# Two reorderings in a three-stage mixer kernel: operands 5 and 6 of a pair, and the vector work of the first MLP

## The chip, the core and the metric

The kernel runs on one core of a Trainium2 chip. The metric is the device time of one execution in microseconds (us). TensorE multiplies matrices into PSUM; VectorE (DVE), ScalarE (ACT) and GpSimd (POOL) do the elementwise work; SyncE (SP) issues the DMAs. Each engine takes its instructions strictly in the order in which the program lists them, so an instruction that waits holds up all that stand behind it on its engine.

## What is computed

```python
def _attn_ref(q, k, v):                    # 4 batches, 8 heads, 576 positions, 64 wide
    scores = q @ k.T / sqrt(64)            # kept where 0 <= i - j < 64, else -1e9
    attn = exp(scores - max) / (sum + 1e-9)
    return attn @ v

def _moe_ref(x, g_ln, w_ch1, w_ch2):       # first MLP: 512 -> 2048 -> 512
    xn = (x - mean) / sqrt(var + 1e-6) * g_ln
    return x + maximum(xn @ w_ch1, 0) @ w_ch2

def _moe2_ref(x, w_tok1, w_tok2, w_ch1, w_ch2):
    u = x + token_mix(x)                   # along the 576 positions, 256 hidden
    return u + maximum(u @ w_ch1, 0) @ w_ch2   # second MLP: 512 -> 1536 -> 512
```

The output of each stage is the input of the next. Everything is float32, and the weights arrive as 64-bit numbers.

## The kernel before, in words

**Precision.** Each large product is made as three TensorE passes of a rounded type (`PASSES`): a number is split into a high half, written by ScalarE, and a low half, the difference, written by DVE or POOL (`split`, L105; `relu_split`, L364). The passes are high x high, high x low and low x high. Where the text says high half and low half, these two instructions are meant.

**Tiles and blocks.** The 2304 rows are 18 tiles of 128; three tiles make a block (384 columns of a transposed operand), so there are six blocks (`NBLOCKS`).

**First MLP** (`mlp_block`, L392). For block i, TensorE runs 16 steps f. A step is one `mm1` (L378: 12 matmuls into a hidden tile, whose two halves ScalarE and DVE then make, L365 and L366) and one `mm2` (L389: 9 matmuls) for the hidden tile of two steps before (`LAG` = 2). Behind the `mm1` of step f come the hooks of that step: all that prepares the next block. Blocks 1 to 4 take the hooks from `STEPS` (L702), where S, V, T and X stand for the work on one tile of the next block and a digit for which tile (3 is the first of the block after next):

- S (`tile_S`, L246): TensorE scores (L192), DVE maxima (L205), ScalarE exponentials (L213), into `f`.
- T (`tile_T_part`, L254): 16 DVE transposes, L260, of `f` into `pts`; T0*4 is four of them.
- V (`tile_PV`, L268): TensorE multiplies `pts` by the values (L285), DVE scales the result (L291); then `ln_scalar` (L301) centres the tile into `xh` on ScalarE.
- X (`xh_part`, L355): 16 DVE transposes, L359, of `xh` into `xhT`.

At a block's end `after` (L776) scales the three `xhT` into the next block's operand `xnt`.

**Early pieces.** 13 further weight pieces are fetched, narrowed, split and written back to DRAM meanwhile, in rows of the big tile `xs` that are still free (slots 9, 12 and 15). `EARLY` (L682) gives each slot the global steps (16 a block, block 1 starts at 0) at which a piece begins, and `PHASES` how many steps later each phase runs: load (SP), shrink (ScalarE), narrow (two DVE instructions), split (ScalarE and POOL), keep (SP).

**Token mixing** is a list written out by hand, `MIXING` (L56): u is `tok_up`, d is `tok_down` (TensorE, then a DVE addition, L856), r is DVE transposes, x is `x_step` (L897).

**Second MLP.** Two blocks at a time make a pair, three pairs in all. A group (`quad`, L942; six groups q per pair) computes two times two output blocks with seven products instead of eight: product k takes operand `xm[k]` (0 to 6), a sum or difference of the four quarters of the pair's input. The seven operands are made by `x_steps` (L874): four DVE subtractions `subs` (L877, into `t1`, `t2`, a quarter, and `t1` again) and seven splits `puts` (L107 high, L108 low). `subs[3]` overwrites `t1` for operand 6; `puts[5]` and `puts[6]` make operands 5 and 6. The list `lo` says which engine makes each low half. Products alternate between two PSUM banks, `pa` (0, 2, 4, 6) and `pb_` (1, 3, 5). Product 2 goes on in `pa`, which the ScalarE copy `s1` (L930) must have read first; likewise `s5` for product 3, and so on. Behind the products come the down products of the group before (L925, 36 matmuls), with ScalarE's and DVE's halves of the hidden tiles (L936, L939) between them.

```python
            product(pa, 0, a11)
            copy(s1, pa)
            job(0)
            product(pb_, 1, m1)
            copy(s5, pb_)
            job(1)
            product(pa, 2, m2, False)
```

`jobs` (L1000) holds what else is done in a group, by its place: job(k) stands behind product k for k up to 5, job(6) to job(9) behind the four pairs of hidden halves. Before the change the operands of the first pair are all made in the mixing list (x0 to x6), and those of the second and third pair in places 0 to 7 of the last group of the pair before (L1048 to L1056).

Of the kernel before, what the change touches and what calls it, by code (L numbers as in the profile page):

```python
# [12 lines left out]
U32 = mybir.dt.uint32  # L13
# [4 lines left out]
P = 128  # L18
B, H, S, D = 4, 8, 576, 64
DM = 512  # L20
# [4 lines left out]
T1 = 256  # L25
# [28 lines left out]


MIXING = ("u0 u1 y0 u2 d0 d1 y1 u3 d2 d3 y4 k4 r2 d4 r2 y2 k5 d5 r2 d6 y3 r2 d7 r2 t0 d8 r2 u4 w0 r2 u5 n2 t1 r2 x0 u6 x1 "  # L56
          "d9 x2 d10 u7 w1 n3 x3 d11 x4 d12 x5 d13 x6")


LOADS = ("q1 v0 q2 v1 g0 v2 w6")  # L60
# [12 lines left out]
def mixer_kernel(ctx, tc, qT, kT, v, g, wa1, wa2, tok1, tok2, wb1, wb2, out):  # L73
# [26 lines left out]
    def wslot(k, shape, name, dtype=F32R):  # L100

        return wp.tile(shape, dtype, tag=f"w{k}", name=name)
# [7 lines left out]
    def shrink(raw):  # L110

        h_ = raw.rearrange("p (n two) -> p n two", two=2)[:, :, 1].bitcast(F32)
        nc.scalar.activation(out=h_, in_=h_, func=AF.Prelu, scale=2.0 ** -112, alpha=2.0 ** 32)

    def narrow(pairs, psum=True):

        for d, r in pairs:
            w = r.rearrange("p (n two) -> p n two", two=2)
            low = ps_l.tile([P, DM], U32, tag="l", name="low")[:, 0:d.shape[1]] if psum else d
            nc.vector.tensor_scalar(out=low, in0=w[:, :, 0], scalar1=29, scalar2=None, op0=ALU.logical_shift_right)
            nc.vector.scalar_tensor_tensor(out=d, in0=w[:, :, 1], scalar=3, in1=low,
                                           op0=ALU.logical_shift_left, op1=ALU.bitwise_or)
        return [d.bitcast(F32) for d, _ in pairs]
# [280 lines left out]
    with tc.manual_schedule():  # L408
# [270 lines left out]

        EARLY = {9: (-1, 10), 12: (0, 10, 15, 26), 15: (0, 11, 16, 27, 32, 37, 43)}  # L682
        PHASES = ((0, piece_load), (2, piece_shrink), (2, piece_narrow), (3, piece_split), (4, piece_keep))
        pieces = [t1_piece(0), t1_piece(1), t2_piece(0), t2_piece(1), rest_piece()]
        pieces += [w2_piece(q, k) for q in range(HALF - 2) for k in range(2)]
        starts = sorted((g_, x) for x, gs in EARLY.items() for g_ in gs)
        at = collections.defaultdict(list)
        for (g_, x), piece in zip(starts, pieces):
            for d, fn in PHASES:
                at[g_ + d].append((d, fn, x, piece))  # L690

        def early_hooks(g_, hooks):
            for d, fn, x, piece in sorted(at[g_], key=lambda e: -e[0]):
# [4 lines left out]
                else:  # L698
                    hooks.append(call)


        STEPS = ("T0*4", "T0*4", "", "V0 S1", "X0*6 T1*2", "T1*8", "T1*6", "V1 S2 X0*5", "X0*5 T2*4", "T2*8", "T2*4 X1*4",  # L702
                 "V2 S3 X1*5", "X1*7", "X2*8", "X2*8 T3*8")
        done = collections.Counter()


# [190 lines left out]
        def x_step(k):  # L897
            {1: subs0[0], 2: subs0[1]}.get(k, lambda: None)()
            puts0[k]()
            {3: subs0[2], 5: subs0[3]}.get(k, lambda: None)()  # L900

        for op in MIXING.split():
            k = int(op[1:])
# [92 lines left out]
        for p in range(PAIRS):  # L996
            old = acc
            for q in range(HALF):
                n = p * HALF + q
                jobs = collections.defaultdict(list)  # L1000
                if p == 0:
                    if q == 0:
                        for k, t in ((1, 14), (3, 15), (5, 16), (9, 17)):
                            jobs[k].append(lambda t=t: tok_down(t))
                        jobs[9] += [lambda: load_w2(2), lambda: load_w2(3)]
                        more = wslot(15, [P, 2, 2 * DM], "more", U32)
                        wide = {}

                    def w2_raw(q2):
                        for k in range(2):  # L1010
                            f = q2 + k * HALF
                            nc.sync.dma_start(out=more[:, k], in_=wb2[f * P:(f + 1) * P, :].bitcast(U32))

                    def w2_narrow(q2, k):
                        if k == 0:
                            wide[q2] = ap.tile([P, 2, DM], U32, tag="p", name=f"wide{q2}")
                        narrow([(wide[q2][:, k], more[:, k])], False)

                    def w2_split(q2):
                        w2[q2], t_ = wslot(W2_SLOT[q2], [P, 2, 2, DM], f"w2_{q2}"), wide.pop(q2).bitcast(F32)  # L1020
                        for k in range(2):
                            split(w2[q2][:, k, 0], w2[q2][:, k, 1], t_[:, k], nc.gpsimd)

                    for m in range(2):
                        q2 = HALF - 2 + m
                        if q == m:
                            jobs[9].append(lambda q2=q2: w2_raw(q2))
                        if q == m + 1:
                            for k in range(2):
                                jobs[6].append(lambda k=k: shrink(more[:, k]))  # L1030
                                jobs[7 + 2 * k].insert(0, lambda q2=q2, k=k: w2_narrow(q2, k))
                        if q == m + 2:
                            jobs[5].append(lambda q2=q2: w2_split(q2))
                if 2 <= n + 1 < PAIRS * HALF:
                    jobs[0].append(lambda n=n: load_w1(n + 1))
                if p < PAIRS - 1:
                    if q == 0:
                        ux = qkv.rearrange("p a b n -> p (a b n)").rearrange("p (i c n) -> p i c n", i=2, n=N)
                        per = (6, 7, 7, 6, 6, 0)
                        todo = [(i, k) for i in range(2) for k in range(16)]  # L1040

                    def turn(m, p=p, ux=ux):
                        for i, k in todo[:m]:
                            block_transpose(ux[:, i], 2 * (p + 1) + i, k)
                        del todo[:m]
                    for k in range(per[q]):
                        jobs[5 + k % 5].append(lambda: turn(1))
                    if q == HALF - 1:  # L1048
                        tx = wslot(15, [P, 2, 2, N], f"tx{p}", F32)
                        subs, puts = x_steps(*(ux[:, i, c:c + 2] for i in range(2) for c in (0, 2)), tx[:, 0], tx[:, 1],  # L1050
                                        [nc.gpsimd, nc.vector] * 4)
                        jobs[0] += subs[:2]
                        jobs[3].append(subs[2])
                        for k, m in ((4, 0), (4, 1), (5, 2), (5, 3), (5, 4), (6, 5), (7, 6)):
                            jobs[k].append(puts[m])
                        jobs[6].insert(0, subs[3])  # L1056
                if q == 1:
                    acc = []
                    jobs[3].append(lambda p=p, acc=acc: acc.extend(new_acc(p)))
                for m, k, js in ((0, 8, (3, 4)), (0, 9, (5, 0)), (1, 0, (1, 2))):  # L1060
                    if q == m and p > 0:
                        jobs[k] += [lambda j=j, p=p, old=old: store(2 * TPB * (p - 1) + j, old[j]) for j in js]
                quad(n, old if q == 0 else acc, jobs)
# [54 lines left out]
```

## Time and profile before

| | us |
|---|---|
| median of 3 runs (lowest, highest) | 817.39 (815.83, 817.45) |
| the profiled execution | 816.4 |
| its span | 814.5 |
| TensorE busy | 798.4 |
| DVE, ScalarE, POOL busy | 535.5, 332.2, 174.7 |

The first MLP with the attention takes the time from the start to about 477 us, token mixing to about 518 us, and the second MLP the rest. TensorE's granted clock was 1.00 in every stretch of 20 us but the last (0.99). In a timeline, a row is a run of like instructions: start, time, engine, line, operation, output and inputs, and the count; in brackets, the idle time of the engine just before and what ended it. Ends of matmuls are modelled, so one run may end a little after the next has begun.

### The profile page before, as it was taken

What the parts mean: (1) busy time and instruction counts of PE and PEld (TensorE: products, weight loads), DVE (VectorE), ACT (ScalarE), POOL (GpSimd) and SP (SyncE); (2) the same over time, 40 slices, a digit from 0 to 9 for tenths busy, and PEclk for the clock granted to TensorE, in tenths of its full rate; (3) what the DMA queues carried; (4) which work ended last, traced back from release to release, by engine and by line L of the source; (5) the groups of instructions that cost most, each with busy time, mean ns of one, the idle gap of its engine ahead of it and who ended that gap; (6) DMA issues with size and microseconds to landing.
All of it is one profiled execution on the core that took longest, in us unless ns stands there. A gap on an engine that the chain in (4) does not pass through costs nothing.

```text
span 814.5 us, 13225 instructions
## 1 busy us (share of the span) xinstructions
PE 798.4 (98%) x4914; PEld 708.9 (87%) x4914; DVE 535.5 (66%) x1326; ACT 332.2 (41%) x852; POOL 174.7 (21%) x181
## 2 busy tenths in 40 slices
PE   8999999999999999999999999899999999999998
PEld 6788888889889888888999888789988998898997
DVE  5898697887889688777677337766465544732223
ACT  6887634444343344342254532333242222522221
POOL 4655401011001000000033933301231000400000
PEclk9999999999999999999999999999999999999999
DMA  9888324342322323121059516166240734235202
GB/s 339 271 293 273 101 93 135 111 168 85 110 78 78 111 85 110 35 81 56 1 135 354 201 40 245 52 245 232 93 176 4 257 117 156 91 112 218 109 1 78
DMA packets 35152, 112.67 MB, mean 138 GB/s; under 512 B 5008, under 2 KB 6544, under 8 KB 31632
## 3 DMA queue, kind: packets, MB, share of 16 engines
q1 hardware_dynamic: 34944, 111.56, 39.6%
q8 instruction: 39, 0.64, 0.3%
q10 hardware_dynamic: 144, 0.26, 0.1%
q14 instruction: 25, 0.20, 0.1%
HBM read 88.87 MB, written 22.41 MB: 137 GB/s over the span
## 4 chain that ended last, share of the span: by engine, by line
PE 76%; DVE 14%; ACT 5%; issue 2%; DMA 0%; POOL 0%; DVEq 0%; ACTq 0%
PE acca L389 18%; PE ha L378 17%; PE accb L925 15%; PE prod L916 15%; DVE pts L260 4%; PE th L839 3%; PE td L853 2%; PE o L285 2%; ACT f L213 2%; PE s L192 2%; DVE xhT L359 2%; DVE hTa L366 1%; PE accb L1074 1%; DVE xm L108 1%; PE pt L228 1%
## 5 line engine op out<-in xcount | busy, mean ns | idle before, releaser
L378 PE MATMUL ha<-xnt,wa 128*128 128x384 f32 x1152 | 216.9, 337 | 0.8 <-POOL wa L108 0.5
L389 PE MATMUL acca<-wa,hTa 128*128 128x512 f32 x864 | 215.8, 396 | 0.3 <-DVE hTa L366 0.3
L378 PEld LDWEIGHTS ha<-xnt,wa 128*128 128x128 f32 x1152 | 203.9, 188 | 9.5 <-DVE xnt L343 1.2
L389 PEld LDWEIGHTS acca<-wa,hTa 128*128 128x128 f32 x864 | 159.2, 188 | 33.3 <-issue 2.4
L925 PE MATMUL accb<-w,hx 128*128 128x512 f32 x612 | 142.2, 390 | 0.0
L925 PEld LDWEIGHTS accb<-w,hx 128*128 128x128 f32 x612 | 114.6, 188 | 23.2
L365 ACT ACTIVATE hTa<-ha 128x384 fp32r<-128x384 f32 x96 | 46.8, 488 | 186.7 <-PE ha L378 182.8
L366 DVE SCALAR_TENSOR_TENSOR hTa<-ha,hTa 128x384 fp32r<-128x384 f32 x96 | 53.2, 554 | 68.6 <-ACT hTa L365 67.8
L260 DVE STREAM_TRANSPOSE pts<-f 32x256 f32<-32x256 f32 x192 | 83.7, 436 | 3.1
L933 POOL TENSOR_TENSOR s<-s,s 128x384 f32<-128x384 f32 x18 | 18.2, 1014 | 228.3 <-ACT s L930 228.3
L916 PE MATMUL prod<-xm,w1b 128*128 128x384 f32 x324 | 59.9, 336 | 5.8 <-ACT s L930 5.8
L930 ACT ACTIVATE s<-prod 128x384 f32<-128x384 f32 x72 | 35.0, 492 | 68.1 <-PE prod L916 62.4
L916 PEld LDWEIGHTS prod<-xm,w1b 128*128 128x128 f32 x324 | 56.2, 188 | 7.4 <-ACT s L930 7.2
L939 DVE SCALAR_TENSOR_TENSOR hx<-s,hx 128x384 fp32r<-128x384 f32 x54 | 33.1, 616 | 44.8 <-ACT hx L936 44.7
L933 DVE TENSOR_TENSOR s<-prod,s 128x384 f32<-128x384 f32 x36 | 20.1, 557 | 63.4 <-PE prod L916 63.4
L359 DVE STREAM_TRANSPOSE xhT<-xh 32x128 f32<-32x128 f32 x192 | 57.8, 301 | 2.8
L936 ACT ACTIVATE hx<-s 128x384 fp32r<-128x384 f32 x54 | 27.9, 523 | 67.9 <-PE accb L925 66.7
L108 POOL TENSOR_TENSOR wa<-tmp,wa 128x512 fp32r<-128x512 f32 x32 | 41.5, 1312 | 34.0 <-ACT wa L107 32.3
L213 ACT ACTIVATE f<-f,mx 128x128 f32<-128x128 f32 x120 | 46.3, 387 | 1.2 <-DVE mx L205 1.2
L309 POOL TENSOR_SCALAR mv<-mv 128x1 f32<-128x1 f32 x13 | 2.6, 197 | 181.9 <-ACT xhT L308 181.8
L916 PE MATMUL prod<-xm,w1a 128*128 128x384 f32 x216 | 40.9, 336 | 0.0
L916 PEld LDWEIGHTS prod<-xm,w1a 128*128 128x128 f32 x216 | 38.0, 188 | 0.1
(150 smaller groups left out, 955.5 us busy)
## 6 DMA issues: line engine op xcount, KB each, us to landing
xs<-in_wa SPq DMA_DIRECT2D x32, 512.0 KB, 4.6
w1b<-kept SPq DMA_DIRECT2D x16, 1024.0 KB, 7.2
w1a<-kept SPq DMA_DIRECT2D x16, 768.0 KB, 4.8
qkv<-in_v SPq DMA_DIRECT2D x28, 256.0 KB, 3.1
qkv<-in_wb SPq DMA_DIRECT2D x12, 512.0 KB, 4.5
kept<-w1b SPq DMA_DIRECT2D x6, 1024.0 KB, 8.2
kept<-w1a SPq DMA_DIRECT2D x6, 768.0 KB, 6.2
xs<-in_wb SPq DMA_DIRECT2D x8, 512.0 KB, 4.7
```

The lines of the kernel that those rows point to most:

```text
L108: lo_engine.tensor_tensor(out=dst_lo, in0=src, in1=dst_hi.bitcast(F32), op=ALU.subtract)
L213: nc.scalar.activation(out=f_[:, h], in_=f_[:, h], func=AF.Exp, scale=-1.0, bias=mx[:, h], accum_out=sm[:, h])
L260: nc.vector.transpose(out=s_[32 * b:32 * b + 32, :, 32 * a:32 * a + 32], in_=f_[32 * a:32 * a + 32, :, 32 * b:32 * b + 32])
L359: nc.vector.transpose(out=uts[t][32 * b:32 * b + 32, :, 32 * a:32 * a + 32], in_=s_)
L365: nc.scalar.activation(out=dst_hi, in_=src, func=AF.Relu)
L366: nc.vector.scalar_tensor_tensor(out=dst_lo, in0=src, scalar=0.0, in1=dst_hi.bitcast(F32), op0=ALU.max, op1=ALU.subtract)
L378: nc.tensor.matmul(h_, lhsT=w[:, a, c * P:(c + 1) * P], rhs=src[c][:, b], start=n == 0, stop=n == 3 * KD - 1)
L389: nc.tensor.matmul(acc[j], lhsT=t_[:, a, j * P:(j + 1) * P], rhs=ws[f][:, 2 + b], start=f == first and n == 0, stop=f == last and n == 2)
L916: nc.tensor.matmul(dst, lhsT=w_[:, a, c * P:(c + 1) * P], rhs=xm[m][:, c, b], start=first and n == 0, stop=n == 5, skip_group_check=True)
L925: nc.tensor.matmul(acc[j], lhsT=hx[role][:, a, (j % TPB) * P:(j % TPB + 1) * P], rhs=w2[q][:, k, b], start=q == 0 and role in ("21", "12") ...
L930: nc.scalar.activation(out=dst, in_=src, func=AF.Copy)
L933: eng.tensor_tensor(out=dst, in0=x, in1=y, op=ALU.add)
```

## The change

The mixing list loses x5 and x6. For every pair, `subs[3]`, `puts[5]` and `puts[6]` are put at places 0, 1 and 3 of the first group that uses the operands, ahead of what stands there. For pairs two and three, operand 4 moves from place 5 to place 6 of the last group before, and the low halves of operands 5 and 6 change engines (5 from DVE to POOL, 6 from POOL to DVE). The buffer `more`, which takes the memory of `ut`, is taken when it is first loaded, since `ut` is now read in that group. In the first MLP the steps of S and V stay where they are, transposes move between steps, an early piece's numbers name the step of its shrink and narrow (loaded two steps before), and its split is done at least one step later and not before step 4 of a block.

```diff
@@ -54,7 +54,7 @@
 
 
 MIXING = ("u0 u1 y0 u2 d0 d1 y1 u3 d2 d3 y4 k4 r2 d4 r2 y2 k5 d5 r2 d6 y3 r2 d7 r2 t0 d8 r2 u4 w0 r2 u5 n2 t1 r2 x0 u6 x1 "
-          "d9 x2 d10 u7 w1 n3 x3 d11 x4 d12 x5 d13 x6")
+          "d9 x2 d10 u7 w1 n3 x3 d11 x4 d12 d13")
 
 
 LOADS = ("q1 v0 q2 v1 g0 v2 w6")
@@ -679,15 +679,16 @@
 
 
 
-        EARLY = {9: (-1, 10), 12: (0, 10, 15, 26), 15: (0, 11, 16, 27, 32, 37, 43)}
-        PHASES = ((0, piece_load), (2, piece_shrink), (2, piece_narrow), (3, piece_split), (4, piece_keep))
+        EARLY = {9: (1, 13), 12: (2, 12, 18, 28), 15: (2, 12, 18, 28, 34, 40, 45)}
         pieces = [t1_piece(0), t1_piece(1), t2_piece(0), t2_piece(1), rest_piece()]
         pieces += [w2_piece(q, k) for q in range(HALF - 2) for k in range(2)]
         starts = sorted((g_, x) for x, gs in EARLY.items() for g_ in gs)
         at = collections.defaultdict(list)
         for (g_, x), piece in zip(starts, pieces):
-            for d, fn in PHASES:
-                at[g_ + d].append((d, fn, x, piece))
+            late = max(4 - g_ % FA, 1)
+            for n, (d, fn) in enumerate(((-2, piece_load), (0, piece_shrink), (0, piece_narrow), (late, piece_split),
+                                         (late + 1, piece_keep))):
+                at[g_ + d].append((n, fn, x, piece))
 
         def early_hooks(g_, hooks):
             for d, fn, x, piece in sorted(at[g_], key=lambda e: -e[0]):
@@ -699,8 +700,8 @@
                     hooks.append(call)
 
 
-        STEPS = ("T0*4", "T0*4", "", "V0 S1", "X0*6 T1*2", "T1*8", "T1*6", "V1 S2 X0*5", "X0*5 T2*4", "T2*8", "T2*4 X1*4",
-                 "V2 S3 X1*5", "X1*7", "X2*8", "X2*8 T3*8")
+        STEPS = ("T0*4", "T0*4", "", "V0 S1 X0*6", "T1*6", "T1*8", "T1*2 X0*5", "V1 S2 X0*5", "T2*8", "T2*8", "X1*9",
+                 "V2 S3 X1*7", "X2*6", "X2*10", "T3*8")
         done = collections.Counter()
 
 
@@ -897,7 +898,7 @@
         def x_step(k):
             {1: subs0[0], 2: subs0[1]}.get(k, lambda: None)()
             puts0[k]()
-            {3: subs0[2], 5: subs0[3]}.get(k, lambda: None)()
+            {3: subs0[2]}.get(k, lambda: None)()
 
         for op in MIXING.split():
             k = int(op[1:])
@@ -1000,21 +1001,24 @@
                 jobs = collections.defaultdict(list)
                 if p == 0:
                     if q == 0:
+                        subs, puts = subs0, puts0
                         for k, t in ((1, 14), (3, 15), (5, 16), (9, 17)):
                             jobs[k].append(lambda t=t: tok_down(t))
                         jobs[9] += [lambda: load_w2(2), lambda: load_w2(3)]
-                        more = wslot(15, [P, 2, 2 * DM], "more", U32)
-                        wide = {}
+                        wide, more = {}, []
 
                     def w2_raw(q2):
+                        if not more:
+                            raw = wslot(15, [P, 2, 2 * DM], "more", U32)
+                            more.extend(raw[:, k] for k in range(2))
                         for k in range(2):
                             f = q2 + k * HALF
-                            nc.sync.dma_start(out=more[:, k], in_=wb2[f * P:(f + 1) * P, :].bitcast(U32))
+                            nc.sync.dma_start(out=more[k], in_=wb2[f * P:(f + 1) * P, :].bitcast(U32))
 
                     def w2_narrow(q2, k):
                         if k == 0:
                             wide[q2] = ap.tile([P, 2, DM], U32, tag="p", name=f"wide{q2}")
-                        narrow([(wide[q2][:, k], more[:, k])], False)
+                        narrow([(wide[q2][:, k], more[k])], False)
 
                     def w2_split(q2):
                         w2[q2], t_ = wslot(W2_SLOT[q2], [P, 2, 2, DM], f"w2_{q2}"), wide.pop(q2).bitcast(F32)
@@ -1027,12 +1031,15 @@
                             jobs[9].append(lambda q2=q2: w2_raw(q2))
                         if q == m + 1:
                             for k in range(2):
-                                jobs[6].append(lambda k=k: shrink(more[:, k]))
+                                jobs[6].append(lambda k=k: shrink(more[k]))
                                 jobs[7 + 2 * k].insert(0, lambda q2=q2, k=k: w2_narrow(q2, k))
                         if q == m + 2:
                             jobs[5].append(lambda q2=q2: w2_split(q2))
                 if 2 <= n + 1 < PAIRS * HALF:
                     jobs[0].append(lambda n=n: load_w1(n + 1))
+                if q == 0:
+                    for k, fn in ((0, subs[3]), (1, puts[5]), (3, puts[6])):
+                        jobs[k].insert(0, fn)
                 if p < PAIRS - 1:
                     if q == 0:
                         ux = qkv.rearrange("p a b n -> p (a b n)").rearrange("p (i c n) -> p i c n", i=2, n=N)
@@ -1048,12 +1055,11 @@
                     if q == HALF - 1:
                         tx = wslot(15, [P, 2, 2, N], f"tx{p}", F32)
                         subs, puts = x_steps(*(ux[:, i, c:c + 2] for i in range(2) for c in (0, 2)), tx[:, 0], tx[:, 1],
-                                        [nc.gpsimd, nc.vector] * 4)
+                                        [nc.gpsimd, nc.vector, nc.gpsimd, nc.vector, nc.gpsimd, nc.gpsimd, nc.vector])
                         jobs[0] += subs[:2]
                         jobs[3].append(subs[2])
-                        for k, m in ((4, 0), (4, 1), (5, 2), (5, 3), (5, 4), (6, 5), (7, 6)):
+                        for k, m in ((4, 0), (4, 1), (5, 2), (5, 3), (6, 4)):
                             jobs[k].append(puts[m])
-                        jobs[6].insert(0, subs[3])
                 if q == 1:
                     acc = []
                     jobs[3].append(lambda p=p, acc=acc: acc.extend(new_acc(p)))
```

## Rows read from the trace of the kernel before

**Rows 1.** The page, the span and its part 1: busy us, share of span, instructions.

```profile
span 814.5 us, 13225 instructions
...
PE 798.4 (98%) x4914; PEld 708.9 (87%) x4914; DVE 535.5 (66%) x1326; ACT 332.2 (41%) x852; POOL 174.7 (21%) x181
```

**Rows 2.** Busy time by stretch: blocks 1 to 4, length first, then engines' busy us, clock, DMA.

```profile
106.30:182.63 76.33, 74.43 (x530) 66.24 (x528) 63.60 (x194) 33.39 (x103) 9.63 (x12) 1.00 0.37 120
182.63:257.13 74.50, 74.09 (x529) 66.32 (x528) 62.41 (x195) 31.40 (x99) 7.38 (x10) 1.00 0.29 96
257.13:330.90 73.77, 73.77 (x529) 66.14 (x528) 60.91 (x193) 30.15 (x97) 6.10 (x9) 1.00 0.25 85
330.90:404.67 73.77, 73.77 (x503) 66.30 (x502) 55.35 (x167) 23.84 (x75) 2.23 (x6) 1.00 0.15 47
```

**Rows 3.** Timeline of TensorE, block 1.

```profile
137.81 1.15 PE L285 MATMUL o<-qkv,pts 128*64 128x64 f32 x30 [1.58 <-DVE pts L260]
...
180.89 1.90 PE L389 MATMUL acca<-wa,hTa 128*128 128x512 f32 x7 [0.32 <-DVE hTa L366]
```

**Rows 4.** Timeline of DVE, block 1, steps 4 to 7.

```profile
127.03 0.56 DVE L366 SCALAR_TENSOR_TENSOR hTa<-ha,hTa 128x384 fp32r<-128x384 f32 x1 [5.12 <-ACT hTa L365]
127.50 1.86 DVE L359 STREAM_TRANSPOSE xhT<-xh 32x128 f32<-32x128 f32 x6
...
135.07 2.69 DVE L260 STREAM_TRANSPOSE pts<-f 32x256 f32<-32x256 f32 x6
```

**Rows 5.** Timeline of ScalarE, block 1, end of step 3.

```profile
125.10 0.38 ACT L213 ACTIVATE f<-f,mx 128x128 f32<-128x128 f32 x1
...
125.49 1.14 ACT L107 ACTIVATE xs<-xs 128x512 fp32r<-128x512 f32 x2
```

**Rows 6.** Timeline of DVE, end of block 1.

```profile
174.11 2.52 DVE L359 STREAM_TRANSPOSE xhT<-xh 32x128 f32<-32x128 f32 x8
...
180.28 0.56 DVE L366 SCALAR_TENSOR_TENSOR hTa<-ha,hTa 128x384 fp32r<-128x384 f32 x1
```

**Rows 7.** Timeline of TensorE, second MLP.

```profile
523.60 2.37 PE L916 MATMUL prod<-xm,w1b 128*128 128x384 f32 x12 [2.29 <-ACT s L930]
...
597.48 1.23 PE L916 MATMUL prod<-xnt,w1a 128*128 128x384 f32 x6
...
604.79 8.36 PE L925 MATMUL accb<-w,hx 128*128 128x512 f32 x36
613.00 1.23 PE L916 MATMUL prod<-xnt,w1a 128*128 128x384 f32 x6
...
616.74 3.42 PE L916 MATMUL prod<-xm,w1b 128*128 128x384 f32 x18 [1.47 <-ACT s L930]
...
711.79 3.39 PE L916 MATMUL prod<-xm,w1b 128*128 128x384 f32 x18 [1.44 <-ACT s L930]
```

**Rows 8.** Timeline of ScalarE around the first groups of pairs one and two.

```profile
522.32 0.84 ACT L107 ACTIVATE xm<-t0x 128x768 fp32r<-128x768 f32 x1 [2.81 <-DVE t0x L877]
...
599.79 0.49 ACT L930 ACTIVATE s<-prod 128x384 f32<-128x384 f32 x1 [0.55 <-PE prod L916]
...
612.21 0.85 ACT L107 ACTIVATE xm<-tx 128x768 fp32r<-128x768 f32 x1 [2.79 <-DVE tx L877]
...
616.20 0.87 ACT L930 ACTIVATE s<-prod 128x384 f32<-128x384 f32 x2 [2.31 <-DVE hx L939]
```

**Rows 9.** Timeline of DVE around the start of pair two.

```profile
602.41 0.95 DVE L877 TENSOR_TENSOR qkv<-qkv 128x768 f32<-128x768 f32 x1
604.90 2.23 DVE L108 TENSOR_TENSOR xnt<-tx,xnt 128x768 fp32r<-128x768 f32 x1 [1.54 <-ACT xnt L107]
...
612.96 3.14 DVE L939 SCALAR_TENSOR_TENSOR hx<-s,hx 128x384 fp32r<-128x384 f32 x3
```

**Rows 10.** Timeline of POOL, last group of pair one.

```profile
604.46 1.86 POOL L108 TENSOR_TENSOR xnt<-qkv,xnt 128x768 fp32r<-128x768 f32 x1
606.28 2.56 POOL L108 TENSOR_TENSOR xm<-tx,xm 128x768 fp32r<-128x768 f32 x1
```

## What the change does to the time

> **What bounds the kernel now.** I read the busy shares first, then the stretches of the first MLP block by block, then TensorE's own timeline for the idle time in brackets, and only then, for each gap, the queues of the engines named in it. The busy shares [rows 1] say that TensorE works for 798.4 of 814.5 us: whatever the change does, it can only take from the remaining 16 us, and part of those are the start and the last stores, which it does not touch. A change of order pays only where TensorE waits.
>
> There are two places. In the first MLP the four blocks that also prepare the next block do the same TensorE work, but last 76.33, 74.50, 73.77 and 73.77 us [rows 2]. The last two have no idle TensorE time, so 73.77 is the price of the work, and the first two lose 2.56 and 0.73 us, 3.29 in sum. The timeline names the waits of the first: the probabilities-times-values products (L285) wait 1.58 us for the DVE transposes of their tile (L260), and the last second-layer products (L389) 0.32 us for a hidden tile [rows 3]. The bracketed idle time is a little less than the loss, since matmul ends are modelled and overlap the next start.
>
> The second place is the third product of the first group of each of the three pairs of the second MLP. It writes the bank that the copy s1 has to read first, and it waits 2.29, 1.47 and 1.44 us for that ScalarE copy [rows 7]. In a group without a wait the seven products take (604.79 - 597.48) / 7 = 1.044 us each. The second pair begins at 613.00, so its third product was due at 615.09 and started at 616.74: 1.65 us lost, 0.18 over the bracket. With the same 0.18 the three are 2.47, 1.65 and 1.62, together 5.74 us. Why the copy is late stands in two queues. For the first pair ScalarE stood 2.81 us waiting for a DVE subtraction into t0x, then made the high half of operand 6, and only then came to the copies. For the second it waited 2.79 us for the subtraction into tx, and then 2.31 us more for DVE's low halves [rows 8], three of which took 3.14 us and ended at 616.1 [rows 9]. So the work of operands 5 and 6, queued ahead of the group, delays a copy that needs neither.
>
> **The change, part by part.** *Operands 5 and 6.* The subtraction into t1, both halves of operand 5 and both of operand 6 leave the end of the pair before (for the first pair, the mixing list) and go behind products 0, 1 and 3 of the group that uses them; nothing is added. Ahead of the group, ScalarE loses two activations of 0.84 us [rows 8] and DVE a subtraction and a low half, 0.95 us each when alone and over 2 beside a POOL instruction [rows 9]. The copies then wait for TensorE only: 5.74 us come free.
>
> What takes their place is worked out for the second pair, with the group starting at 613.00. The subtraction follows DVE's last low half and runs beside products 1 and 2. The copy of product 1 started 2.31 us after the group's start in the undisturbed group (599.79 against 597.48) [rows 7, 8], so at 615.31; after it, 0.39 later since it is pipelined (0.87 for two against 0.49 for one), ScalarE makes high half 5 until 615.70 + 0.84 = 616.54. The copy s2 queued behind it is due at 616.35 and slips by 0.1; it ends at 616.95, and product 4, which overwrites that bank, comes at 617.18: hidden with 0.2 to spare. POOL's low half 5 takes 1.86 or 2.56 us [rows 10] and so ends at 618.5 or 619.1, and product 5 wants it at its second matmul, 613.00 + 5 x 1.044 + 0.17 = 618.4. The stall is 0.1 or 0.7 us. I take 0.1, because the 1.86 belongs to the half that started 0.44 us ahead of the DVE instruction beside it (which took 2.23 in place of 0.95), and the 2.56 to one that started while DVE held on [rows 9, 10]; here low half 5 starts first. Low half 6 on DVE follows the addition of product 3 and that POOL instruction: 618.5 + 0.95 = 619.4, when product 6 wants it at its second matmul (613.00 + 6 x 1.044 + 0.17 = 619.4): nothing, with 0.7 as the bound if low half 5 takes 2.56. The third pair is alike, so 0.2 us come back. Behind high half 6 on ScalarE stands the copy of product 4, and behind low half 6 on DVE the addition of product 5; both are due after 618.4 and wait for nothing but their product. In the first pair a token-mixing product (`tok_down`, six matmuls) stands behind each of products 1, 3 and 5, so product 5 comes later still by two of these: nothing comes back. The net of this part is 5.74 - 0.2 = 5.5 us.
>
> The Trainium skill's page "SBUF — State Buffer" (section "Who interferes with whom") says that GpSimd and a DVE instruction with two inputs in SBUF lock the port they share for a whole instruction, and that the one which started first is not slowed. The rows agree (1.86 beside 2.23); by that rule the stall at product 5 is the 0.1, by a sharing of the port it would be the 0.7, and the total 1.2 us more over two pairs.
>
> *Low halves change engine, operand 4 goes one step later.* Low half 5 goes to POOL and 6 to DVE. Operand 4 moves behind the first high half of the products; its POOL low half queued behind two others anyway (the second of them ran to 606.28 + 2.56 = 608.84 [rows 10]), and product 4 of the next group comes at 617.18. Nothing. *The buffer `more`* is taken later, with its loads, which stand at the same place of SP's queue: nothing.
>
> *Order of the first MLP's DVE work.* In step 3 DVE stood 5.12 us waiting for a ScalarE high half [rows 4], which was queued behind the exponentials and two early splits of 1.14 us [rows 5]. Then came 1.86 us of X0 transposes, and tile 1's 16 transposes ended at 137.76, after TensorE had arrived at 137.81 - 1.58 = 136.2. The change puts the six X0 transposes into that idle time, ahead of the wait, and moves the splits behind the high half. The low half then ends at about 127.59 - 1.14 = 126.5; 16 transposes at 2.69 / 6 = 0.45 us and two low halves of 0.57 between them give 126.5 + 7.2 + 1.1 = 134.8, or 1.4 us before TensorE comes. If the idle time did not cover X0, the 1.86 would come back and the stall would be 0.5. The 1.58 us of this wait go, and the 0.73 of the second block, which has the same steps and two pieces. At the block's end the late low half starts at 180.28, behind eight X2 and eight T3 transposes [rows 6]. Steps 11 to 14 now hold 23 X transposes in place of 28, so it comes 5 x 0.315 = 1.6 us sooner, against a loss of at most 2.56 - 1.58 = 0.98: gone, and the lower bound is that all of it stays. *Early pieces.* Their 13 loads, shrinks, narrows, splits and keeps are the same in number; narrows move by one step at most. Three splits now meet in step 4 of the first block, 3 x 0.57 = 1.7 us of ScalarE and their POOL halves, behind the high half that mattered and while DVE still transposes; the next high half slips, but its DVE partner is behind those transposes. The keeps, one or two steps later on SP, have the operand loads of step 7 behind them, three steps off. Nothing. This part is worth 3.3 us, at least 0 and at most 3.3.
>
> **The sum.** 5.5 + 3.3 = 8.8 us. The profiled execution took 816.4 (span 814.5), so it would take 807.6. It lies 1.0 below the median of the runs shown, 817.39; against that, 808.6.
>
> **Rivals.** *A, the low halves collide:* low half 5 takes 2.56, low half 6 follows it, and products 5 and 6 wait 0.7 us more in two pairs. The row of 2.56 speaks for it, the free POOL at that time against it. 810.0. *B, the first MLP's stall stays:* the transposes of tile 1 end as late as before because the exponentials, not X0, set them. The 1.4 us margin is against it. 808.6 + 3.3 = 811.9. *C, the change only moves the waits:* what product 2 gains comes back at product 5, because operand 5 is late there by as much (5.7 us), and transposes brought forward in one step are paid for in a later one (3.3 us): 817.4. For it speaks that no work is taken away, against it that DVE and ScalarE stood idle where the work now goes. *D, slower:* the chain of operands 5 and 6 does not run beside the products but in a line. Subtraction 2.2, high half 0.84, low half 2.56, and for operand 6 high 0.84 and low 2.2 follow one another, 8.6 us; only the 3.1 us of three products cover it. TensorE then stands 5.5 us in each pair, 16.5 in sum against the 0.2 forecast: 808.6 + 16.3 = 824.9. It is slower once the stall is over 0.1 + 8.8 / 3 = 3.0 us a pair. Against it: the steps are on three engines, and each finds its own free in the rows.
>
> **How the numbers follow.** Forecast 0.70 (808.6), A 0.10, B 0.09, C 0.05, D 0.06. A difference under 0.2%, 1.6 us, about the spread of the runs shown, can't be told from none. Faster: 0.70 + 0.10 + 0.09 = 0.89; same: C, 0.05; slower: D, 0.06. The range takes in the runs' spread below (808.6 - 1.8) and A and B above with a little spread: 806.8 to 812.2.
>
> **What would show it.** Right: the four blocks at 73.8 us each; no wait of L285 for L260 after the first block; the third product of each pair's first group 2.09 us after its start (in the first pair right behind its token product); DVE's wait in step 3 shrunk by 1.9 us of X0 transposes; at most 0.2 us of idle time at product 5 of pairs two and three. Wrong: idle time ahead of L916 released by POOL or DVE L108, over 0.5 us a pair (A, and D if over 3); blocks one and two still over 74.4 (B); the copy s1 still waiting for DVE (C).

## The result, and the profile after

The changed kernel takes 806.81 us (median of 4 runs, 806.6 to 806.88), the kernel before 816.61 us (median of 4, 815.8 to 817.45): a ratio of 0.9879, 95% interval 0.9862 to 0.9897. That is 9.8 us less, where the prediction had 8.8. The time lies 1.8 us under the 808.6 forecast, at the very edge of the range. Of these 1.8 us, 0.78 are the kernel before itself: its median was 817.39 us over three runs and is 816.61 with a fourth. The other 1.0 us is how much more the change takes than forecast, and the experiments look for its cause.

The page of the changed kernel, its span and part 1 (compare [rows 1]):

```profile
span 804.8 us, 13221 instructions
...
PE 795.7 (99%) x4914; PEld 707.9 (88%) x4914; DVE 530.1 (66%) x1326; ACT 332.6 (41%) x852; POOL 174.9 (22%) x181
```

The stretches of blocks 1 to 4 of the changed kernel, which answer to [rows 2]:

```profile
105.54:179.31 73.77, 73.77 (x529) 66.18 (x528) 64.27 (x199) 33.13 (x103) 9.55 (x12) 1.00 0.38 124
179.31:253.08 73.77, 73.77 (x529) 66.17 (x528) 62.22 (x194) 31.30 (x99) 7.48 (x10) 1.00 0.29 97
253.08:326.86 73.78, 73.78 (x530) 66.17 (x528) 60.32 (x191) 30.23 (x97) 6.08 (x9) 1.00 0.24 85
326.86:400.63 73.77, 73.77 (x503) 66.35 (x502) 53.38 (x162) 23.83 (x75) 2.22 (x6) 1.00 0.15 47
```

All four blocks now last what the third lasted before: the 3.29 us are gone, all of them. DVE's timeline of block 1 shows how (the same steps as [rows 4]):

```profile
120.78 1.88 DVE L359 STREAM_TRANSPOSE xhT<-xh 32x128 f32<-32x128 f32 x6 [0.59 <-ACT xhT L308]
124.24 0.56 DVE L366 SCALAR_TENSOR_TENSOR hTa<-ha,hTa 128x384 fp32r<-128x384 f32 x1 [1.59 <-ACT hTa L365]
...
132.19 0.89 DVE L260 STREAM_TRANSPOSE pts<-f 32x256 f32<-32x256 f32 x2
```

The idle 5.12 us ahead of the low half have become 0.59, six transposes and 1.59 more. Tile 1's last transposes end at 133.08. TensorE's timeline has the values product at 135.14, 2.06 us later and with no idle time in brackets, where it waited 1.58 us before [rows 3]:

```profile
135.14 1.15 PE L285 MATMUL o<-qkv,pts 128*64 128x64 f32 x32
```

TensorE's timeline of the second MLP before the change, the starts of each pair's first group and of the group after it, as far as [rows 7] has not got them:

```profile
517.66 1.23 PE L916 MATMUL prod<-xnt,w1a 128*128 128x384 f32 x6
...
525.81 1.55 PE L853 MATMUL td<-h,t 128*128 128x512 f32 x6
...
534.48 1.23 PE L916 MATMUL prod<-xnt,w1a 128*128 128x384 f32 x6
...
630.31 1.23 PE L916 MATMUL prod<-xnt,w1a 128*128 128x384 f32 x6
...
708.08 1.23 PE L916 MATMUL prod<-xnt,w1a 128*128 128x384 f32 x6
...
725.31 1.23 PE L916 MATMUL prod<-xnt,w1a 128*128 128x384 f32 x6
```

The same in the changed kernel, with more of the groups themselves:

```profile
513.61 1.23 PE L917 MATMUL prod<-xnt,w1a 128*128 128x384 f32 x6
...
517.11 2.25 PE L917 MATMUL prod<-xm,w1b 128*128 128x384 f32 x12
...
527.86 1.23 PE L917 MATMUL prod<-xnt,w1a 128*128 128x384 f32 x6
...
606.34 1.23 PE L917 MATMUL prod<-xnt,w1a 128*128 128x384 f32 x6
...
608.45 3.29 PE L917 MATMUL prod<-xm,w1b 128*128 128x384 f32 x18
611.57 2.51 PE L917 MATMUL prod<-xm,w1a 128*128 128x384 f32 x12
613.92 8.36 PE L926 MATMUL accb<-w,hx 128*128 128x512 f32 x36
622.12 1.23 PE L917 MATMUL prod<-xnt,w1a 128*128 128x384 f32 x6
...
699.86 1.23 PE L917 MATMUL prod<-xnt,w1a 128*128 128x384 f32 x6
...
715.64 1.23 PE L917 MATMUL prod<-xnt,w1a 128*128 128x384 f32 x6
```

Product 2 no longer waits (517.11 and 608.45 carry no bracket). From one group's start to the next, the first groups of the three pairs last 14.25, 15.78 and 15.78 us, where the profiled execution of before had 16.82, 17.31 and 17.23: 2.57, 1.53 and 1.45 less, 5.55 in sum. An undisturbed group lasts 15.54, so 0.24 us a pair have come back, at product 5: products 5 and 6 begin at 611.57 and end their turn at 613.92, 2.35 later in place of 2.09. POOL's and DVE's timelines show the two low halves:

```profile
610.01 1.84 POOL L108 TENSOR_TENSOR xm<-qkv,xm 128x768 fp32r<-128x768 f32 x1 [5.30 <-issue]
```

```profile
611.27 1.39 DVE L108 TENSOR_TENSOR xm<-tx,xm 128x768 fp32r<-128x768 f32 x1
```

Low half 5 ends at 611.85, when product 5's second matmul was due at 611.57 + 0.17 = 611.74. That is 0.11 of the 0.24 us; the rows don't place the rest, but all of it goes when operand 5 is made sooner (below). Low half 6 takes 1.39 us in place of 0.95: it starts 0.58 us ahead of POOL's end.

Of the 9.7 us between the two spans, these rows hold 3.29 + 5.55 = 8.84. Another 0.76 is the opening, the time up to block 1: block 1 begins at 105.54 us, before the change at 106.30 [rows 2], though nothing of the program is different up to there.

### The profile page after: what moved, and what is told of

Read it like the earlier page. It is cut to its first block, busy times and chain, and to the rows that moved or that the text cites. A ratio compares the mean times of both kernels' runs of the same rounds, so it can differ in the third digit from the quotient of the medians.

```text
span 804.8 us, 13221 instructions
## 1 busy us (share of the span) xinstructions
PE 795.7 (99%) x4914; PEld 707.9 (88%) x4914; DVE 530.1 (66%) x1326; ACT 332.6 (41%) x852; POOL 174.9 (22%) x181
## 4 chain that ended last, share of the span: by engine, by line
PE 95%; DVE 2%; ACT 1%; DMA 0%; POOL 0%; issue 0%; DVEq 0%
PE acca L389 24%; PE ha L378 24%; PE accb L926 17%; PE prod L917 16%; PE td L854 3%; PE th L840 3%; PE o L285 2%; PE s L192 2%; PE accb L1080 1%; PE pt L228 1%; DVE tmp L125 1%; DMA xs<-in_wa 0%; ACT f L213 0%; DVE low L124 0%; ACT wa L107 0%; DVE scratch L205 0%
```

## The experiments

A measure that leaves the opening out serves below: from the start of block 1 to the start of the last down products (between L1074 and L1080 of the timelines, by the run). It is 802.98 - 106.30 = 696.68 us in the profile of before and 793.26 - 105.54 = 687.72 in the changed kernel's, 8.96 less.

### The two kernels once more

No edit.

> The kernel before, once more. Theory 1 (the two executions compared differ by 0.76 us in the opening up to block 1 only by chance): the opening of this execution lies anywhere between the 105.5 and 106.3 us seen so far, the blocks last 76.3, 74.5, 73.8 and 73.8 us again, and the three first groups of the pairs 16.8, 17.3 and 17.2 us. Theory 2 (the opening is longer in the kernel before because of its code): block 1 starts at 106.3 us again.

> The changed kernel, once more. Theory 1: the same blocks (73.8 us each) and first groups (14.3, 15.8, 15.8 us), and an opening that may differ from 105.54 us by some tenths. Theory 2: block 1 starts at 105.5 us again. Time 806.8 us, ratio 0.988.

Measured: the kernel before 817.23 us (10 runs, 815.77 to 817.72), against 816.41 of 14 runs of the same kernel beside it; the changed one 806.86 (4 runs, 806.75 to 807.44). Block 1 began at 105.57 us in this execution of the kernel before and at 106.36 in this one of the changed kernel: the opening differs between executions, whatever the kernel, so theory 1 holds. The changed kernel's blocks and groups repeated to 0.03 us, and so did those of before, but for one. Its first group of pair one lasted 18.39 us in place of 16.82. TensorE's timeline of that execution:

```profile
516.94 1.23 PE L916 MATMUL prod<-xnt,w1a 128*128 128x384 f32 x6
...
519.04 1.55 PE L853 MATMUL td<-h,t 128*128 128x512 f32 x6
522.88 3.92 PE L916 MATMUL prod<-xm,w1b 128*128 128x384 f32 x12 [2.28 <-ACT s L930]
526.63 1.55 PE L853 MATMUL td<-h,t 128*128 128x512 f32 x6
...
535.33 1.23 PE L916 MATMUL prod<-xnt,w1a 128*128 128x384 f32 x6
```

The wait is as long as in [rows 7], 2.28 us against 2.29. But from the 12 matmuls behind it to the next row it is 526.63 - 522.88 = 3.75 us, where the first profile has 525.81 - 523.60 = 2.21. The stretches of that execution (length; busy us and count of TensorE, weight loads, DVE, ScalarE, POOL; granted clock; DMA) show the granted clock:

```profile
520.60:522.80 2.20, 0.00 (x0) 0.00 (x0) 1.89 (x3) 1.20 (x3) 0.15 (x1) 1.00 0.00 0
522.80:524.00 1.20, 1.12 (x4) 1.12 (x5) 1.20 (x2) 0.41 (x2) 0.00 (x0) 0.67 0.00 0
524.00:525.00 1.00, 1.00 (x4) 1.00 (x4) 0.04 (x1) 0.05 (x1) 0.00 (x0) 0.50 0.06 16
525.00:526.00 1.00, 1.00 (x5) 1.00 (x5) 0.00 (x0) 0.44 (x1) 0.00 (x0) 0.50 0.00 0
526.00:527.00 1.00, 1.00 (x5) 0.96 (x5) 0.10 (x1) 0.00 (x0) 0.00 (x0) 0.69 0.00 0
527.00:528.00 1.00, 1.00 (x6) 0.81 (x5) 0.46 (x1) 0.00 (x0) 0.00 (x0) 1.00 0.00 0
```

TensorE stood idle, with the granted clock still at 1.00; just after it had begun to work again, the clock went from 1.00 to 0.50 (2.4 to 1.2 GHz), and it came back some three microseconds later. The stretches there in the first profile of before read 1.00 throughout. So one wait of one length costs two different amounts, and the execution that the prediction read was a cheap one.

The times alone tell the two kinds apart. In all, 30 of 50 times of the kernel before, over all experiments, lie above 816.9 us. For 46 of the 50 the mean granted clock of the execution is on record: it is 0.997 or 0.998 in all 28 above 816.9 us, and 1.000 in all 18 below. A median of this kernel moves by most of a microsecond with the share of dear executions in it, as the 817.23 and 816.41 show.

### One part alone

The first takes over the steps and the early pieces only, the second the rest of the diff only.

> Only the part on the first MLP (steps and early pieces); operands 5 and 6 are made where the kernel before makes them. Theory 1 (the parts add): blocks of 73.8 us, first groups of 16.8, 17.3 and 17.2 us, 3.3 us under the kernel before: 813.3 us against a median of 816.6, ratio 0.996. Rival (what the first MLP gains comes back in the token mixing, or needs the other part): 815 us or more.

> Only the part on operands 5 and 6; the first MLP is that of the kernel before. Theory 1: blocks of 76.3 and 74.5 us as before, first groups of 14.3, 15.8 and 15.8 us, 5.55 us under the kernel before: 811.1 us, ratio 0.993. Rival (part of the 9.8 us comes from the two together): less than 5 us.

Measured: the first MLP's part 813.38 us (ratio 0.9963, 0.995 to 0.9976), with blocks of 73.77 and first groups of 16.82, 17.32 and 17.30; the part on operands 5 and 6 810.43 us (0.9922, 0.9907 to 0.9936), with blocks of 76.33 and 74.51 and first groups of 14.25, 15.78 and 15.78. In the waits that it was made for, each part does its own and nothing else. Leaving the opening out, they take 3.1 and 5.6 us off, 8.7 together, where the whole change takes 8.96; in the profile of the first MLP's part one group of pair two lasted 15.82 us in place of 15.54, which is most of the difference and has no cause on record. So the parts add. The spread is telling: with the wait of pair one in place, four runs lay between 813.04 and 813.58 and one, the only one with a mean granted clock of 0.997, at 815.02; without it, all four lay within 0.3 us, with a clock of 1.000.

### The wait filled

```diff
                         for k, t in ((1, 14), (3, 15), (5, 16), (9, 17)):
                             jobs[k].append(lambda t=t: tok_down(t))
+                        jobs[1].append(lambda: dummies(13))
```

> The kernel before, with 13 small matmuls on the identity, of no use to the result, put on TensorE behind the first token product of pair one's first group, where it waits 2.3 us for the copy s1. They fill the wait and need nothing. Theory 1 (the wait in the kernel before sometimes takes TensorE's granted clock from 2.4 to 1.2 GHz, which costs another 1.57 us, as in one of the two profiles; that makes the two groups of times of the kernel before, near 816 and near 817.4 us): all times fall in the lower group, 815.6 to 816.6 us, and the first group lasts 16.8 us. Theory 2 (the two groups of times come from elsewhere, such as the opening): still about half of the times above 817 us.

Measured: 816.36 us (ratio 0.9991, 0.9981 to 1.0), and nine of ten times between 815.96 and 816.54, with a mean granted clock of 1.000; beside it, on the same chip, nine of 13 times of the kernel before were above 817. The first group lasted 17.14 us: the matmuls came out as 26 in the trace and ran 2.8 us, 0.3 longer than the wait. TensorE's timeline:

```profile
520.56 3.06 PE L487 MATMUL idle<-ident 128*128 128x128 f32 x26
523.38 2.33 PE L916 MATMUL prod<-xm,w1b 128*128 128x384 f32 x12
```

The medians' ratio by itself is hardly clear of 1; what tells is the count, one dear time of ten against nine of 13. Useless work that lengthens the group by 0.3 us lowers the median by 1.0, because the clock stays up in nine executions of ten. The tenth, 817.84, has a mean granted clock of 0.998 like the dear executions of the kernel before, so the clock fell in it too; it was not profiled, and where it fell stays open.

### The wait put back, alone

The changed kernel with x5 and x6 back in the mixing list, and the moved operands only from the second pair on:

```diff
-          "d9 x2 d10 u7 w1 n3 x3 d11 x4 d12 d13")
+          "d9 x2 d10 u7 w1 n3 x3 d11 x4 d12 x5 d13 x6")
...
-            {3: subs0[2]}.get(k, lambda: None)()
+            {3: subs0[2], 5: subs0[3]}.get(k, lambda: None)()
...
-                if q == 0:
+                if q == 0 and p > 0:
```

> The changed kernel with the mixing list of the kernel before, so that only pair one makes operands 5 and 6 ahead of its first group again; pairs two and three and the first MLP stay as changed. Theory 1 (this wait alone takes the clock down in some executions): the wait of 2.3 us at product 2 is back, and the times fall in two groups again, 2.6 us over the changed kernel (near 809.4 us) and 1.6 us above that (near 811.0 us). Rival (the two groups of the kernel before come from another place, such as the waits of pairs two and three or the first MLP): one group near 809.4 us, as narrow as that of the changed kernel.

Measured: 809.5, 809.59, 810.94, 811.13 and 811.26 us, two groups 1.5 us apart; the mean granted clock is 1.000 in the first two and 0.998 in the other three. The profiled execution was one of the cheap ones, 809.5, its first group 16.82 us and its clock 1.00. With the last experiment this settles it: the wait of pair one makes the two groups of times, by taking the clock down in some executions. The other waits that the change removes are not needed for it: this kernel has none of them, and has the groups. Nor is a dear execution on record where product 2 waits in no pair's first group: in all 36 of the changed kernel and of the versions that share this with it, the mean granted clock is 0.999 or 1.000. Whether the waits of pairs two and three can do it once in a while is open; the version with the wait filled still has them, and has its one dear time.

### One half of the edit of the first MLP undone

First the old `STEPS` with the new pieces, then the new steps with the old `EARLY` and `PHASES`.

> The changed kernel with the old order of steps; the early pieces stay as changed. Theory 1 (two covers for the same wait: splits moved out of ScalarE's way give 1.14 us, and narrows that no longer run beside a POOL split about 1 us): the wait of the values product in block 1 shrinks from 1.58 to at most 0.2 us, that of block 2 is gone, and the end of block 1 keeps up to 0.6 us: 0.3 to 0.8 us over the changed kernel, 807.1 to 807.7. Rival (the order of steps alone is what counts): blocks of 76.3 and 74.5 us, 810.1 us.

> The changed kernel with the old schedule of the early pieces; the order of steps stays as changed. Theory 1: X0 in DVE's idle time alone gives 1.86 us against a wait of 1.58, and the 28 to 23 X transposes free the block's end: blocks of 73.8 to 74.0 us, within 0.2 us of the changed kernel, 806.8 to 807.0. Rival (both halves of the edit are needed, each for its share): 1 us or more over it, 807.9 us.

Measured: with the old steps 808.97 us (0.9898, 0.9884 to 0.9913), with the old pieces 807.59 (0.9882, 0.9866 to 0.9899). With the old pieces every block lasts 73.8 us, as theory 1 had it, and leaving the opening out this version takes 0.2 us more than the changed kernel; its median is 0.6 us above theory 1's upper figure, and its profiled execution had a later opening (block 1 at 106.08 us). With the old steps the values product does not wait either; blocks 1 and 2 last 74.42 and 73.77. DVE's timeline of block 1 with the old steps:

```profile
124.44 0.56 DVE L366 SCALAR_TENSOR_TENSOR hTa<-ha,hTa 128x384 fp32r<-128x384 f32 x1 [4.05 <-ACT hTa L365]
124.91 1.87 DVE L359 STREAM_TRANSPOSE xhT<-xh 32x128 f32<-32x128 f32 x6
...
132.48 2.69 DVE L260 STREAM_TRANSPOSE pts<-f 32x256 f32<-32x256 f32 x6
```

The transposes end at 135.17 and TensorE arrives at 135.33. With the old pieces, DVE's last transposes of tile 1 and TensorE's values product are:

```profile
134.76 0.89 DVE L260 STREAM_TRANSPOSE pts<-f 32x256 f32<-32x256 f32 x2
```

```profile
135.68 1.18 PE L285 MATMUL o<-qkv,pts 128*64 128x64 f32 x32
```

So either half alone removes the wait, but only just: the pieces with 0.16 us to spare, the steps with 0.03. The order of the steps is needed for the block's end, where TensorE still waits 0.33 us for the hidden tile and the block loses 0.65. That is close to what theory 1 said of these blocks, but the time is 1.3 us above its upper figure, and leaving the opening out it is 1.75 us over the changed kernel. Some 0.36 us more in block 3 and 0.27 in each of two groups of the second MLP (15.81 us in place of 15.54) appear in that profile, with no wait beside them; they are not explained.

### Operand 5 later, and sooner

Each run has one of the two new lines in place of the old: the first puts operand 5 later, the second sooner.

```diff
-                    for k, fn in ((0, subs[3]), (1, puts[5]), (3, puts[6])):
+                    for k, fn in ((0, subs[3]), (3, puts[6]), (3, puts[5])):
+                    for k, fn in ((0, subs[3]), (0, puts[5]), (3, puts[6])):
```

> The changed kernel with operand 5 put at place 3 of the first group, just ahead of operand 6, in place of 1. Theory 1 (product 5 waits for POOL's low half of operand 5, which then ends 1.2 us later; operand 6's low half waits for the same POOL instruction and is still in time): the first groups of pairs two and three last 16.8 us in place of 15.8, that of pair one stays at 14.25 us behind its token products, and the time is 2 us over the changed kernel, 808.8 us. Rival (the 0.24 us left at product 5 is not a wait for that half): 15.8 us stay, 806.8 us. If a wait of some 1.2 us also took the clock down, some times would lie 1.6 us higher still.

> The changed kernel with operand 5 put at place 0 of the first group, ahead of the last subtraction, in place of 1. Theory 1: ScalarE makes its high half right behind the copy s1 and POOL ends the low half 1.1 us sooner, so product 5 no longer waits; operand 6's low half no longer waits for POOL: the first groups of pairs two and three last 15.54 us in place of 15.78, 0.5 us under the changed kernel. Rival (the copy s5 behind that high half comes too late for product 3): product 3 waits in place of product 5, 15.8 us or more.

Measured: later, 809.25 us (0.9902, 0.9887 to 0.9916), the first groups of pairs two and three 16.82 and 16.83 us, that of pair one 14.25. Sooner, 806.73 us (0.9875, 0.9862 to 0.9889), 15.54 us in both, with nothing lost at product 5. That is 0.24 us a pair, as theory 1 had it; leaving the opening out, 0.4 us less than the changed kernel, though the medians differ by only 0.1. TensorE's timeline of the later one:

```profile
612.16 0.34 PE L917 MATMUL prod<-xm,w1a 128*128 128x384 f32 x1
613.50 2.20 PE L917 MATMUL prod<-xm,w1a 128*128 128x384 f32 x11 [1.01 <-POOL xm L108]
```

Product 5 does one matmul with the high half and then waits for POOL, as theory 1 had it. Two such waits of 1.01 us spread the times no wider than 0.5 us, with a mean granted clock of 1.000 in all four.

### The wait that is left, and the two together

In the changed kernel one wait of TensorE remains in the second MLP, 0.59 us in the second group:

```diff
-                        per = (6, 7, 7, 6, 6, 0)
+                        per = (6, 7, 7, 6, 6, 0) if p else (0, 8, 8, 8, 8, 0)
```

> The changed kernel with pair two's 32 block transposes done in groups 1 to 4 of pair one, eight in each, and none in group 0. Theory 1 (in the second group product 2 waits 0.6 us for the copy s1, which waits for DVE's last low half, held up by six transposes among the four low halves of a group that has no down products between them): the second group lasts 15.6 us in place of 16.4, 0.8 us under the changed kernel. Rival (the four low halves alone are late): 16.4 us stay.

> The last two together. Theory 1: they add, 1.3 us under the changed kernel, some 805.6 us against 806.9, and a ratio of 0.986 to the kernel before.

Measured: 806.24 us (0.9871, 0.9857 to 0.9884), the second group 15.54 in place of 16.40; with operand 5 sooner as well, 805.92 us (0.9866, 0.985 to 0.9881). Leaving the opening out, 0.7 and 1.2 us less than the changed kernel. DVE's timeline with the transposes moved shows the three last low halves in one run of 1.48 us, where the changed kernel has them 1.17 apart with a transpose between each:

```profile
526.09 0.56 DVE L940 SCALAR_TENSOR_TENSOR hx<-prod,hx 128x384 fp32r<-128x384 f32 x1 [0.88 <-ACT hx L937]
526.57 1.48 DVE L940 SCALAR_TENSOR_TENSOR hx<-s,hx 128x384 fp32r<-128x384 f32 x3
```

The two together are faster than both kernels; the step over the changed kernel, 0.9 us, rests on the rows and on times taken on different chips.

## Why the prediction was right, and where it failed

**The mechanisms held, and their sizes.** The first MLP's part was put at 3.3 us and took 3.29, all of the loss in both blocks; the margin at tile 1 was 2.06 us where 1.4 was expected. That the idle time covers X0, and that the splits' move helps, were both true, and each alone was enough for the values product, by 0.03 and 0.16 us. Operands 5 and 6 were put at 5.5 us and took 5.55 against the profile that the prediction read. What comes back at product 5 was put at 0.1 a pair and measured 0.24. (The working there has a slip: 616.54 + 1.86 is 618.40 and not 618.5, so its own rows gave a stall of 0.01 us.)

**The port of DVE and POOL.** The step that chose 1.86 us over 2.56 for low half 5 measured 1.84: it started first and was not slowed, and the DVE half behind it took 1.39. DVE's extra 0.44 us is 0.14 less than the 0.58 that it overlapped POOL. The two collisions of [rows 9] and [rows 10] come out alike: DVE's 2.23 us are 1.28 over the 0.95 alone for an overlap of 1.42, and POOL's 2.56 are 0.72 over 1.84 for one of 0.85. So in all three the one that started second took nearly the whole overlap longer. The rule cited from the Trainium skill's page "SBUF — State Buffer" (section "Who interferes with whom") agrees with this.

**The rivals.** A (low halves colliding) needed 2.56 us on POOL and fell with the 1.84. B fell with the blocks of 73.77. C fell with the single parts: what was taken away came back only at 0.24 us in each of pairs two and three. D's serial chain did not form; put two places later, operand 5 cost 1.04 us in each of two pairs, well under the 3.0 us a pair at which the prediction had the change turn slower.

**The step that failed** is the price of the first pair's wait. "With the same 0.18 the three are 2.47, 1.65 and 1.62, together 5.74 us" takes what one execution shows as what the wait costs. In the executions of the upper group the same wait also takes the granted clock from 2.4 to 1.2 GHz, and 18.39 - 16.82 = 1.57 us more go. The profile read was a cheap execution, with a late opening (816.4 us); two of the three runs behind the median of 817.39, that median itself and the 817.45, were dear by their times. The prediction saw that these stood 1.0 us apart and set the same 8.8 us against both. By the rows the change takes 8.8 us from a cheap execution and 8.8 + 1.6 = 10.4 from a dear one; by the four times of the result, two of each kind, it is 9.0 and 10.6, and the medians differ by 9.8, between the two. So the 8.8 us set against a dear median was 1.6 us too little. For the same reason the range's lower end had a wrong ground: "the runs' spread below" was taken for noise that the changed kernel would have as well, and the changed kernel does not have it. That 806.81 comes out just at that end is luck. The 0.76 us of the opening between the two profiled executions is chance: both kernels showed both openings.

**The sign** was as forecast: faster, which the prediction gave 0.89.

## What to carry to other kernels

Price a wait of the matrix engine by what runs behind it as well as by its length: look whether the matmuls after it take longer than elsewhere, and at the granted clock there, in more than one execution. Two groups of times in one kernel's runs are a reading in themselves; before forecasting, find out which group the profile belongs to, and what differs; here the mean granted clock of each execution tells. Work that a stage needs late can go into the stage, behind the copies that free its banks, as long as each engine's turn comes before the product that needs it.

## What the runs showed of the hardware

Not expected: behind a wait of 2.28 us the granted clock can go to 0.50 for some three microseconds, in some executions (30 of 50 times of this kernel lay in the upper group) and not in others, for the same instructions. The Trainium skill's page "TensorE: Matmul & The Clock Gate" (section "Part 1: The HAM clock gate") describes a gate that halves the engine's clock after idleness; the stretches above agree on the two levels, with 1.00 and 0.50 and nothing between but in stretches that hold a change. The shorter waits of pairs two and three (1.43 to 1.49 us of idle time) were not seen to do it in the profiles taken: their groups lasted 17.2 to 17.3 us in all four profiles that had them.

Also not expected: the opening. The first 32 score matmuls (L192) took 1.76 us in the first profile of before and 1.10 in that of the changed kernel. TensorE's timelines, before and after:

```profile
1.31 4.64 PE L414 MATMUL idle<-zero 128*128 128x512 f32 x10 [1.31 <-POOL zero L411]
5.88 1.76 PE L192 MATMUL s<-qkv 64*64 64x128 f32 x32
```

```profile
1.31 4.23 PE L414 MATMUL idle<-zero 128*128 128x512 f32 x10 [1.31 <-POOL zero L411]
5.47 1.10 PE L192 MATMUL s<-qkv 64*64 64x128 f32 x32
```

In the second profiles it is the other way round (4.64 and 1.84 us in the changed kernel). The granted clock reads 1.00 in all of these stretches, so the rows don't name a cause; what sets the moment from which the matmuls run faster was not tried.
